# An adaLN block with attention: another list for its first stage, statistics partly on ScalarE, rows of ones by transfers, own banks for block 0's turns, twelve groups

## The chip, the core and the metric

The kernel runs on one core of a Trainium2 chip. Five engines work side by side, each through its own queue in order: TensorE (PE in the rows; PEld is its weight load), VectorE (DVE), ScalarE (ACT), GpSimd (POOL) and SyncE (SP), which issues most transfers. What counts is the device time of one execution in microseconds, the median of several runs.

## What is computed

x has 2048 rows of 512. A condition vector c gives six rows of 512 that shift, scale and gate two halves: attention with 32 heads of 16, and a feed-forward layer of width 1792. Cut to what matters:

```python
mod = (silu(c) @ w_mod).reshape(1, 6, 1, -1)
sa, ca, ga, sb, cb, gb = (mod[:, i] for i in range(6))
h = layernorm(x) * (1 + ca) + sa
qkv = (h @ wqkv).reshape(B, S, 3, 32, 16)
q, k, v = qkv transposed to (3, B, 32, S, 16)
p = softmax(q @ k.T * 16 ** -0.5)          # rows of 2048
x = x + ga * ((p @ v) @ wo)
h = layernorm(x) * (1 + cb) + sb
x = x + gb * (gelu(h @ w1 + b1) @ w2 + b2)
```

## The kernel before, in words

Products are kept exact enough by splitting each fp32 operand into a high and a low part (hi and lo): a product of 512 rows is a *group* of twelve matmuls, eight with the high part of x and four with the low part. The 2048 rows are four blocks of 512.

The kernel has three stages. The **first stage** (about 108 us) norms x, shapes it by the condition, turns it, splits it, and multiplies enough of it by wqkv for the attention to start: 13 groups. From its middle on it also computes row maxima of the scores (tile `mx` on TensorE, reduced on VectorE to `mxp`), which the attention needs ahead of its exponentials. The **attention stage** runs in half-steps: four score matmuls (`e`), four maxima matmuls, four products with v (`pv`), and, on the other half of the array's rows, up to six matmuls of *background* work (`bg`): the groups that the first stage left over, the output projection and the feed-forward layers of the blocks whose attention is done (`block0`, `plan`, `work`). The **tail** does the rest of the background and block 3, on the whole array.

The order of the first stage is written out by hand in `SCRIPT` (line 44), a list of words that the loop at line 569 plays; a word issues its instructions on the engine that it names (.a ScalarE, .v VectorE, .g GpSimd), and each engine keeps that order. The words that the text uses, with block b, tile t, feature chunk f; w is 0 for q, 1 for k, 2 for v:

- Z, W, va, vb: loads of x, of a piece of wqkv, of two pieces of w_mod. hw, lw: high and low part of a weight piece.
- S bt: mean and variance of 128 rows. F, P: add eps, power -0.5 (GpSimd). B: the offset that ScalarE's norm needs. N bt: norm.
- pa, pb, c, ml, md: the modulation product in two halves, its copy, its turn, the columns `modc`.
- T bf: four turns of x into one bank. H bf: shape by `modc` into a tile h32. I, L: high and low part of it.
- G wkb: a group. A, R, D: high part, copy and low part of its result, O: the store, K, Q: loads of keys and queries laid out by heads. U, C: turn and copy of values.
- M: fills a key tile with ones (rows 48, 49 and 112, 113 of each are used as factors for the maxima). X queues two maxima matmuls, x plays a reduction. w: filler matmuls. om, lm: store and load of the maxima rows.

Banks of PSUM are handed out by rings: "pr" (banks 0 and 7) for turns and groups, "mx" for the maxima. A tile waits until the last reader of the one that it replaces is done; the first stage has four h32 tiles (`FIRST`). TensorE's clock is granted by the chip at one of two levels, 1.2 and 2.4 GHz.

Of the kernel before, what the change touches and what calls it, by code (L numbers as in the profile page):

```python
# [45 lines left out]
N02.v ml0 T00 md0 S12 T03 H00.a hw00.g S10 I00.a T01 lw00.g S11 H03.a H01.a bt I03.v hw10.g W01 S13 I01.a T02
lw10.g be F1 L01.v H02.a L03.g W11 L00.v I02.a S22 P1 L02.v G100 S21 B1 N10.a N11.g S20 G000 N13.a R100.v
N12.a A100.v S23 D100.g F2 S31 A000.a P2 O100 T12 D000.v B2 H12.a S30 O000 T10 N22.a I12.g N23.v T13 N20.a
H10.v hw01.g N21.a H13.v T11 I10.g lw01.v I13.a T22 L10.g L12.v H11.a W20 L13.v T20 H22.a I11.g hw11.v T21 K00
H20.a I22.g L11.v I20.a lw11.g T23 H21.v K10 S32 G101 I21.g Q0 H23.v L22.g I23.v Q1 L20.v L23.g G110 L21.v  # L50
A101.a S33 hw20.g lw20.v F3 D101.v P3 R110.a X0*2 O101 A110.a x X0 B3 G200 x D110.g N32.a x N30.a x N31.g O110
N33.a x*2 A200.a X0*2 x X0 G102 K01 x*2 K11 x*3 A102.a X0*2 x X1 T30 D102.v x O102 T32 H30.a x I30.g T33 H32.a
x I32.a x X0*2 H33.a x U200 x I33.g T31 x C200 x O200 K12 L30.g X0*2 x H31.a G010 x K02 I31.g x L32.g x*2
L33.g L31.v A010.a X0*3 x R010.a G103 x D010.g x*2 O010 x*2 R103.a X0*2 x X0 A103.a G203 x D103.g x*2 O103 x*2
A203.a X0*2 x X0 G201 x*4 K03 x A201.a X0*2 x X0 K13 U201 x*2 pa1 C201 x O201 va2 pb1 x*2 vb2 X0 c1.v X0*2 x
ml1 x G111 md1 x*4 A111.a X0*2 R111.v X0 G112 x D111.g x*2 O111 x*2 A112.a X0 x X0 R112.a pa2 x D112.g x pb2 x
O112 x c2.a X1*2 x X1 mb0 x om x mb1 me0.a x U203 me1.a x*2 C203 X1*2 x X1 O203 G202 x*3 lm x*2 A202.a w1 X1
w1 X1 x w1 X1 U202 x*2 C202 x O202 x*2
# [1164 lines left out]
```

## Time and profile before

| what | us |
|---|---|
| median of 3 runs (1736.97 to 1739.30) | 1738.71 |
| the profiled execution, its time | 1738.16 |
| its span, first to last instruction | 1736.3 |
| first stage | 0 to 107.8 |
| attention stage | 107.8 to 1614.2 |
| tail | 1614.2 to 1736.3 |
| busy: PE, DVE, ACT, POOL | 1710.8, 1375.2, 1241.8, 685.0 |

The shares of the whole span (PE 99%) hide that the stages have different limits, so they are read stage by stage. A row of the timeline is: start, duration, engine, line, operation, output and inputs, count, and in brackets how long the engine had been idle and who ended that. A matmul's duration runs from its issue to its result; the distance from one to the next is shorter, and the chain of waits shows that.

### The profile page before, as it was taken

Reading aid. Unit: us, or ns where it says so; the run is one execution under the profiler, and the core shown is the slowest. Engines: PE = TensorE matmul, PEld = TensorE weight load, DVE = VectorE, ACT = ScalarE, POOL = GpSimd, SP = SyncE. Lnnn points to the kernel's source line nnn. Section 1 sums busy time; section 2 is a strip of 40 time slices with the busy share of each in tenths; the row PEclk is TensorE's granted clock in tenths of the full one; section 3 lists DMA queues with packets and bytes.
Section 4 is the critical chain, followed back from the end, with each engine's and each line's share of the span. In section 5 each row is a group of like instructions: output and inputs, shape, how many; then the busy total and the mean of one; then the engine's idle time right before and its main releaser. Section 6 shows DMA issues by size and latency. Waiting matters only on the chain.

```text
span 1736.3 us, 32537 instructions
## 1 busy us (share of the span) xinstructions
PE 1710.8 (99%) x12121; PEld 891.1 (51%) x12121; DVE 1375.2 (79%) x2298; ACT 1241.8 (72%) x2379; POOL 685.0 (39%) x688
## 2 busy tenths in 40 slices
PE   7999999999999999999999999999999999999999
PEld 6654444444444444444445444444445444444777
DVE  7998888888888888888889888888888888860332
ACT  3357778778777778778777778777877778778231
POOL 7333434435121256404631356404631356525310
PEclk8999999999999999999999999999999999999999
DMA  8646776767447534335454444335364344323554
GB/s 292 205 142 200 221 218 182 236 179 223 125 136 206 125 86 117 94 85 136 113 168 106 124 114 105 94 81 166 100 174 114 101 132 114 97 66 111 195 156 166
DMA packets 137130, 251.90 MB, mean 145 GB/s; under 512 B 25854, under 2 KB 45324, under 8 KB 136972
## 3 DMA queue, kind: packets, MB, share of 16 engines
q1 hardware_dynamic: 135712, 248.19, 50.3%
q8 instruction: 96, 1.57, 0.4%
q10 hardware_dynamic: 1260, 1.63, 0.3%
q14 instruction: 62, 0.51, 0.1%
HBM read 188.49 MB, written 61.28 MB: 144 GB/s over the span
## 4 chain that ended last, share of the span: by engine, by line
PE 91%; DVE 4%; ACT 2%; POOL 1%; DMA 1%; issue 1%; SPq 0%; ACTq 0%; POOLq 0%; DVEq 0%
PE bg L274 46%; PE pv L667 29%; PE e L637 11%; PE mx L387 3%; DVE mxp L392 2%; ACT p L642 1%; PE pr L274 1%; PE o L274 1%; PE warm L438 1%; DVE hTlo L481 1%; DVE bst L235 0%; ACT h L849 0%; DMA qst<-m 0%; PE mx L333 0%; PE bg L847 0%
## 5 line engine op out<-in xcount | busy, mean ns | idle before, releaser
L392 DVE TENSOR_REDUCE mxp<-mx 128x1 f32<-128x512 f32 x2048 | 1269.4, 682 | 201.4 <-PE mx L387 182.5
L642 ACT ACTIVATE p<-e 128x512 f32<-128x512 f32 x2032 | 1064.4, 605 | 308.1 <-PE e L637 292.8
L387 PE MATMUL mx<-kh,qst 48*128 48x512 f32 x2048 | 873.3, 441 | 1.9 <-DVE mxp L392 0.4
L637 PE MATMUL e<-qst,kh 50*128 50x512 f32 x2032 | 754.6, 419 | 7.0 <-ACT p L642 6.3
L667 PE MATMUL pv<-p,vg 128*32 128x512 f32 x4096 | 546.6, 605 | 0.0
L637 PEld LDWEIGHTS e<-qst,kh 50*128 50x128 f32 x2032 | 373.7, 186 | 148.7 <-ACT p L642 141.8
L387 PEld LDWEIGHTS mx<-kh,qst 48*128 48x128 f32 x2048 | 368.6, 185 | 21.1 <-DVE mxp L392 16.2
L274 PE MATMUL bg<-w,g 64*128 64x512 f32 (+1 forms) x1044 | 277.8, 404 | 0.0
L274 PEld LDWEIGHTS bg<-w,g 64*128 64x128 f32 (+1 forms) x1044 | 183.0, 185 | 142.7 <-ACT p L642 103.3
L274 PE MATMUL bg<-pchi,w 64*128 64x512 f32 (+1 forms) x656 | 194.5, 416 | 2.1 <-ACT p L642 2.0
L274 PEld LDWEIGHTS bg<-pchi,w 64*128 64x128 f32 (+1 forms) x656 | 109.0, 184 | 150.3 <-ACT p L642 102.2
L274 PE MATMUL bg<-hThi,wqkv 64*128 64x512 f32 x560 | 167.4, 418 | 0.3 <-ACT p L642 0.3
L274 PEld LDWEIGHTS bg<-hThi,wqkv 64*128 64x128 f32 x560 | 92.8, 184 | 118.9 <-ACT p L642 106.3
L667 PEld LDWEIGHTS pv<-p,vg 128*32 128x32 f32 x4096 | 81.4, 108 | 125.4 <-issue 117.6
L884 POOL TENSOR_SCALAR s<-s 128x512 f32<-128x512 f32 x40 | 59.8, 1496 | 137.4 <-ACT s L882 127.0
L903 POOL TENSOR_TENSOR x<-y,x 128x512 f32<-128x512 f32 x28 | 35.9, 1281 | 144.3 <-ACT y L902 139.3
L274 PE MATMUL bg<-pclo,w 64*128 64x512 f32 (+1 forms) x328 | 88.6, 389 | 0.0
L872 DVE TENSOR_TENSOR g<-h,g 128x512 fp32r<-128x512 f32 x16 | 11.6, 723 | 91.5 <-PE bg L274 62.7
L274 PE MATMUL bg<-hTlo,wqkv 64*128 64x512 f32 x280 | 76.4, 392 | 0.0
L819 POOL TENSOR_TENSOR x<-y,x 128x512 f32<-128x512 f32 x12 | 15.4, 1282 | 140.9 <-ACT y L816 114.8
L274 PEld LDWEIGHTS bg<-pclo,w 64*128 64x128 f32 (+1 forms) x328 | 60.5, 184 | 12.3
L274 PE MATMUL bg<-wo,pchi 64*128 64x512 f32 x192 | 64.8, 417 | 0.0
(160 smaller groups left out, 1331.9 us busy)
## 6 DMA issues: line engine op xcount, KB each, us to landing
kh<-qk SPq DMA_DIRECT2D x256, 192.0 KB
w<-w1s SPq DMA_DIRECT2D x56, 512.0 KB
w<-w2s SPq DMA_DIRECT2D x53, 512.0 KB
vg<-v SPq DMA_DIRECT2D x64, 332.0 KB
qk<-parts SPq DMA_DIRECT2D x32, 512.0 KB
qst<-qk SPq DMA_DIRECT2D x64, 192.0 KB
qk<-parts SPq DMA_DIRECT2D x32, 256.0 KB
ou<-osb SPq DMA_DIRECT2D x32, 256.0 KB
```

What stands on the lines that cost most here:

```text
L274: return te.matmul(ps, term[0][r], term[1][r], start=i == 0, stop=i == n - 1)
L387: te.matmul(ps, qst[u][r0 : r0 + KR, p, qc * P : (qc + 1) * P], kh(u, kr // 2)[r0 : r0 + KR, p, (kr % 2) * TB : (kr % 2 + 1) * TB], start= ...
L392: ins = ve.tensor_reduce(mxp[u][:, hc, kr : kr + 1], ps, axis=AX.X, op=ALU.max, negate=True)
L438: te.matmul(warm[:, :P], ident, ident, start=True, stop=True)
L481: e.tensor_tensor(hT[b][1][:, f], keep.pop(("H", b, f)), hT[b][0][:, f].bitcast(F32), op=ALU.subtract)
L637: te.matmul(ps, kh(u, kc // 8)[r0 : r0 + KX, p, (kc % 8) * P : (kc % 8 + 1) * P], qst[u][r0 : r0 + KX, p], start=True, stop=True)
L642: saw(ac.activation(t, ps, AF.Exp, scale=SCALE))
L667: te.matmul(cur["ps"][32 * j : 32 * (j + 1)], vg[u][:, kc, j * VW : j * VW + 32], pt.pop(4 * s + j), start=kc == 0, stop=kc == NKC - 1)
L819: gp.tensor_tensor(x2[t], y, x2[t], op=ALU.add)
L872: ve.tensor_tensor(g[:, 1], h, g[:, 0].bitcast(F32), op=ALU.subtract)
L884: gp.tensor_scalar(s, s, 1.0, None, op0=ALU.add)
L903: later(4, lambda: gp.tensor_tensor(x2[t], y, x2[t], op=ALU.add))
```

## The change

The list is replaced by another one, and four pieces around it change. `S` takes an engine: on ScalarE it is a copy and a squaring of the rows, each with its sum, and a small scaling; its output goes to a scratch tile of h32. Of the sixteen, S10, S30 and S23 go to ScalarE. `M` is now two transfers of two rows each out of the key tile that is filled at the start, in place of a memset of the whole tile; three tiles are filled so. Block 0's turns take banks 1, 2, 5 and 6 of a ring of their own. G112 leaves the list, and `plan` takes it up as background work.

```diff
+S2 = D ** -0.5
 SCRIPT = """
-va0 vb0 Z1 W00 bl W10 Z2 S01 Z3 M3.g S02 S00 S03 M4.g M1.v pa0 w7 va1 F0 P0 pb0 w4 N01.g N00.v N03.v c0.a vb1
+va0 vb0 W00 Z1 bl Z3 W10 S00.v Z2 S01.v M1 M4 S02.v M3 S03.v F0 P0 B0 N00.a N02.v N03.v pa0 w7 N01.v T01 T03 T00 T02 pb0 w4
...
     ring("pr", (0, 7))
+    ring("t0", (1, 2, 5, 6))
...
+    def stat(b, t, e):
+
+        rows = xin[b][:, t]
+        if e is not ac:
+            return ln_stat(mv1[b], t, rows)
+        junk, m = stage("h32"), small.tile([P, 1], F32, tag="m1", name="m1")
+        ac.activation(junk, rows, AF.Copy, scale=S2 / D, accum_out=m)
+        ac.activation(junk, rows, AF.Square, scale=-S2, bias=m, accum_out=mv1[b][:, t, 1:2])
+        ac.activation(mv1[b][:, t, 0:1], m, AF.Copy, scale=1 / S2)
...
     def turn_x(b, f):
-        keep["T", b, f] = ps = take("pr")
+        keep["T", b, f] = ps = take("pr" if b else "t0")
...
+    def ones(i):
+        for r0 in (KR, 64 + KR):
+            sy.dma_start(khalf[i][r0 : r0 + 2].bitcast(F32), khalf[2][r0 : r0 + 2].bitcast(F32))
...
-        "S": lambda b, t: ln_stat(mv1[b], t, xin[b][:, t]), "F": add_eps, "P": power, "B": offset, "N": norm1,
+        "S": stat, "F": add_eps, "P": power, "B": offset, "N": norm1,
...
-        "M": lambda i, e: e.memset(khalf[i].bitcast(F32), 1.0),
-        "w": filler,
+        "M": ones, "w": filler,
...
-        plan = [(1, 1, [3]), (2, 1, [0, 1, 2, 3])]
+        plan = [(1, 1, [2, 3]), (2, 1, [0, 1, 2, 3])]
```

ScalarE's queue from its first modulate on, before (h is the shaped chunk, hThi its high part, xin the rows of x, of block 0 to 3 by their numbers 234, 295, 303, 308; parts and pf are copies of a group's result):

```order
L474 ACTIVATE h_374<-pr,modc 128x512
L190 ACTIVATE hThi_214<-h_374 128x512
L474 ACTIVATE h_390<-pr,modc 128x512
L474 ACTIVATE h_392<-pr,modc 128x512
L190 ACTIVATE hThi_214<-h_392 128x512
L563 ACTIVATE b_h<-pr 128x14
L474 ACTIVATE h_414<-pr,modc 128x512
L190 ACTIVATE hThi_214<-h_414 128x512
L461 ACTIVATE xin_295<-xin_295,nb,rs_257 128x512 x3
L190 ACTIVATE parts<-pr 128x512
L474 ACTIVATE h_491<-pr,modc 128x512
```

The same stretch after; block 1 is now xin_297, block 3 xin_301 and block 2 xin_308:

```order
L190 ACTIVATE hThi_214<-h_410 128x512
L455 ACTIVATE h_417,m_418<-xin_297 128x512
L456 ACTIVATE h_417,mv_253<-xin_297,m_418 128x512
L457 ACTIVATE mv_253<-m_418 128x1
L455 ACTIVATE h_440,m_441<-xin_301 128x512
L190 ACTIVATE pf<-pr 128x512
L190 ACTIVATE parts<-pr 128x512
L455 ACTIVATE h_462,m_463<-xin_308 128x512
L456 ACTIVATE h_462,mv_254<-xin_308,m_463 128x512
L457 ACTIVATE mv_254<-m_463 128x1
L473 ACTIVATE xin_297<-xin_297,nb,rs_257 128x512
L190 ACTIVATE parts<-pr 128x512
```

Three statistics stand where three norms of block 1 stood; of those norms one is left, behind the third statistic (the rows of the second that only repeat are left out).

TensorE's queue from the first group to the second batch of maxima, before (wqkv_232 is the piece of k, wqkv_221 that of q, wqkv_222 the second piece of k, wqkv_224 that of v; hThi and hTlo 214 to 217 are blocks 0 to 3 high):

```order
L274 MATMUL pr<-hThi_214,wqkv_232 128x512 x8
L274 MATMUL pr<-hThi_214,wqkv_221 128x512 x8
L468 MATMUL pr<-ident,xin_295 128x128 x16
L468 MATMUL pr<-ident,xin_303 128x128 x16
L274 MATMUL pr<-hThi_215,wqkv_232 128x512 x8
L274 MATMUL pr<-hThi_214,wqkv_222 128x512 x8
L387 MATMUL mx<-kh_189,qst 128x512 x6
L274 MATMUL pr<-hThi_214,wqkv_224 128x512 x8
```

and after:

```order
L230 MATMUL pr<-wm_197,s_m 32x512 x4
L447 MATMUL pr<-ident 128x128 x7
L480 MATMUL t_347<-ident,xin_234 128x128 x4
L230 MATMUL pr<-wm_198,s_m 32x512 x4
L274 MATMUL pr<-hThi_214,wqkv_221 128x512 x8
L274 MATMUL pr<-hThi_214,wqkv_232 128x512 x8
L480 MATMUL pr<-ident,xin_297 128x128 x16
L480 MATMUL pr<-ident,xin_308 128x128 x16
L274 MATMUL pr<-hThi_215,wqkv_232 128x512 x8
L388 MATMUL mx<-kh_189,qst 128x512 x6
L274 MATMUL pr<-hThi_216,wqkv_232 128x512 x8
```

Block 0's turns moved ahead of the second half of the modulation product, and G110 (wqkv_222) moved from before the first maxima to behind them (the four low-part matmuls of each group, and three more turns of block 0, are left out).

TensorE's queue where the tail begins, behind the last `pv`, before and after (pchi and pclo are the shaped rows of block 2, w a weight piece in the attention stage's ring of tiles, wt one in a tile that exists only in the tail):

```order
L667 MATMUL pv<-p,vg 32x512 x8
L274 MATMUL bg<-pchi_5322,w_22566 128x512 x8
L274 MATMUL bg<-pchi_5322,w_22629 128x512 x8
L274 MATMUL bg<-w_22693,g 128x512 x3
L274 MATMUL bg<-w_22754,g 128x512 x3
L274 MATMUL bg<-w_22814,g 128x512 x3
L274 MATMUL bg<-w_22875,g 128x512 x3
```

```order
L682 MATMUL pv<-p,vg 32x512 x8
L274 MATMUL bg<-pchi_5485,w_22642 128x512 x8
L274 MATMUL bg<-pchi_5485,w_22673 128x512 x8
L274 MATMUL bg<-pchi_5485,w_22734 128x512 x8
L274 MATMUL bg<-w_22794,g 128x512 x3
L274 MATMUL bg<-w_22855,g 128x512 x3
L274 MATMUL bg<-w_22915,g 128x512 x3
L274 MATMUL bg<-wt_22966,g 128x512 x3
```

The tail begins with three first-layer groups where it began with two, and the fourth weight piece behind them is one that is loaded in the tail (the low-part matmuls are left out).

## Rows read from the trace of the kernel before

**Rows 1.** Windows by stage: busy us (and count) by engine, then clock, DMA.

```profile
18.30:48.60 30.30, 22.90 (x96) 16.31 (x93) 29.25 (x50) 14.56 (x22) 26.89 (x25) 0.83 0.81 256
48.60:107.80 59.20, 58.25 (x293) 36.24 (x292) 55.89 (x95) 18.62 (x34) 15.83 (x17) 1.00 0.64 203
107.80:1614.20 1506.40, 1495.41 (x11105) 728.29 (x11104) 1240.25 (x2068) 1179.10 (x2279) 613.75 (x610) 1.00 0.49 136
1614.20:1736.30 122.10, 118.02 (x522) 96.04 (x520) 40.03 (x65) 27.43 (x41) 17.65 (x17) 1.00 0.52 183
```

**Rows 2.** Timeline of PE: turns, G101's high part, first maxima.

```profile
17.90 1.18 PE L468 MATMUL pr<-ident,xin 128*128 128x128 f32 x8
...
30.30 0.60 PE L468 MATMUL pr<-ident,xin 128*128 128x128 f32 x4
...
41.12 3.75 PE L274 MATMUL pr<-hThi,wqkv 128*128 128x512 f32 x8 [1.13 <-DVE h L476]
...
48.62 0.96 PE L387 MATMUL mx<-kh,qst 48*128 48x512 f32 x6
```

**Rows 3.** Timeline of DVE: a run of reductions.

```profile
58.14 7.85 DVE L392 TENSOR_REDUCE mxp<-mx 128x1 f32<-128x512 f32 x13
```

**Rows 4.** Chain of waits (start, us, what): one group, issue to issue.

```profile
71.33 3.00 PE pr L274 x12
```

**Rows 5.** Timelines of DVE and POOL: memsets of key tiles.

```profile
9.33 1.76 DVE L564 MEMSET kh<- 128x2048 f32 x1 [0.38 <-issue]
...
5.21 3.54 POOL L564 MEMSET kh<- 128x2048 f32 x2
```

**Rows 6.** Timeline of SP: the first weight load into a tile of the tail.

```profile
1621.38 0.38 SPq L782 DMA_DIRECT2D wt<-w2s  x1
```

**Rows 7.** Chain of waits: from the second modulation product to modc.

```profile
14.38 1.04 PE pr L230 x8
...
18.08 0.16 DVE modc L540
```

**Rows 8.** Groups, 18.3 to 48.6: count, busy us, mean ns, idle.

```profile
L235 DVE BATCH_NORM_STATS2 bst<-xin 128x6 f32<-128x512 f32 x12 | 8.1, 677 | 0.0
...
L481 POOL TENSOR_TENSOR hTlo<-h,hThi 128x512 fp32r<-128x512 f32 x4 | 6.3, 1586 | 0.8 <-PE pr L468 0.4 <-DVE hThi L192 0.4
...
L474 ACT ACTIVATE h<-pr,modc 128x512 f32<-128x512 f32 x8 | 6.0, 771 | 3.3 <-PE pr L468 2.5 <-POOL hTlo L481 0.7
...
L461 ACT ACTIVATE xin<-xin,nb,rs 128x512 f32<-128x512 f32 x6 | 4.5, 806 | 4.8 <-POOL nb L456 4.8
L192 POOL CAST hThi<-h 128x512 fp32r<-128x512 f32 x5 | 3.9, 797 | 0.0
...
L190 ACT ACTIVATE hThi<-h 128x512 fp32r<-128x512 f32 x5 | 3.2, 632 | 0.3
...
L476 DVE TENSOR_SCALAR h<-pr,modc 128x512 f32<-128x512 f32 x4 | 3.1, 798 | 0.0
...
L463 DVE TENSOR_SCALAR xin<-xin,mv,rs 128x512 f32<-128x512 f32 x1 | 0.5, 516 | 0.0
...
L563 ACT ACTIVATE b_h<-pr 128x14 f32<-128x14 f32 x1 | 0.2, 166 | 0.0
```

**Rows 9.** Windows of 2 us, PE alone: busy, clock, DMA.

```profile
32.00:34.00 2.00, 1.09 (x8) 1.00 1.02 381
...
42.00:44.00 2.00, 2.00 (x6) 0.50 1.06 227
...
46.00:48.00 2.00, 2.00 (x10) 1.00 0.01 3
```

**Rows 10.** Chain of waits: a store's landing, a load's landing.

```profile
48.52 4.65 DMA qk<-parts
...
54.03 3.46 DMA kh<-qk
```

**Rows 11.** Timeline of PE in the tail: full matmuls.

```profile
1619.80 11.72 PE L274 MATMUL bg<-w,g 128*128 128x512 f32 x51
```

More of the change, by code (lines that the diff above doesn't have):

```diff
@@ L44 @@
 SCRIPT = """
-va0 vb0 Z1 W00 bl W10 Z2 S01 Z3 M3.g S02 S00 S03 M4.g M1.v pa0 w7 va1 F0 P0 pb0 w4 N01.g N00.v N03.v c0.a vb1
[L46 to L58, printed above, removed]
+va0 vb0 W00 Z1 bl Z3 W10 S00.v Z2 S01.v M1 M4 S02.v M3 S03.v F0 P0 B0 N00.a N02.v N03.v pa0 w7 N01.v T01 T03 T00 T02 pb0 w4
+c0.v hw00.g ml0 lw00.g md0 H03.a H00.v H02.a I03.g W11 S13.v I00.a I02.g S11.v bt be L00.g L02.v H01.a S12.v I01.a
@@ new lines @@
+L03.g S10.a L01.v G000 S33.v hw10.g S30.a F1 S31.v P1 S32.v R000.a lw10.g A000.a F3 S21.v S23.a S20.v D000.g W20 G100
+S22.v B1 O000 F2 P2 N13.a N10.v N11.v N12.v N22.g A100.a N21.v T10 D100.v H10.a N20.v O100 T13 I10.a T12 N23.g H13.v
+Q0 H12.v I13.a T11 Q1 L10.v I12.a H11.a L13.g T20 L12.v T23 H20.a I11.v P3 H23.a K00 T22 H22.a I23.v T21 L11.g K10
+I22.a G101 I20.a L22.v B3 L23.g N32.a N33.v H21.a N30.v L20.g I21.a X0*2 x X0 N31.a x L21.g G102 R101.a x A101.a x
+D101.g x*2 hw20.g A102.a X0 O101 X0 x X0 R102.a T31 x D102.g H31.a x X0 x I31.a hw11.g O102 T30 x H30.a X0 x lw11.g
@@ new lines @@
+T32 x H32.a X1 K01 x T33 I30.g I32.a x W01 X1 H33.a x K11 G110 L30.g x I33.a K12 x L32.g x K02 x L31.g lw20.v R110.a
+X0 vb1 X0*2 va1 hw01.a x G201 A110.a lw01.g x*3 D110.g x*2 A201.a X0 L33.g O110 X0 x X0 G103 x*5 A103.a X0 R103.v X0*2
+x D103.g G200 x*2 O103 x*3 A200.a X0*2 x X0 pa1 x va2 x X0 pb1 x U200 c1.a K03 x X0 C200 x ml1 vb2 O200 x K13 x X0 x
+X0 G010 x*5 R010.a X0 md1 X0 x X0 A010.a pa2 x D010.g x X0 pb2 x O010 U201 c2.a x X0 x C201 mb1 x O201 x me1.a X0 x X0
+mb0 x*2 me0.a X0 x G111 x*4 R111.a A111.v X1*3 x D111.g om G202 x*2 O111 x*3 A202.a X1 lm X1 x X1 U202 x G203 C202 x*2
@@ L59 @@
+O202 x*2 A203.a w1 X1 w1 X1 x w1 X1 U203 x C203 x X1 x O203 x*4
 """
@@ L372, in block_kernel @@
     xc, red, mrows = [0, 0], {}, set()
-    xorder = [int(t[1]) for t in SCRIPT.split() if t[:2] in ("X0", "X1") for _ in range(int(t[3:] or 1))]
+    xorder = [int(t[1]) for t in SCRIPT.split() if t[:2] in ("X0", "X1", "y0", "y1")
+              for _ in range(int(t[3:]) if "*" in t else 1)]
     xorder = [(u, xorder[:n].count(u)) for n, u in enumerate(xorder)]
```

## The prediction

> **What bounds the kernel now.** I first cut the span into stages by the busy time of each engine [rows 1]. The attention stage (107.8 to 1614.2 us) and the tail behind it are TensorE's: 1495.4 of 1506.4 and 118.0 of 122.1 us busy. The change leaves their code alone but for one group, so what it can win lies in the first 107.8 us. There the bound moves. From 18.3 to 48.6 VectorE is busy 29.25 of 30.3 us and TensorE 22.9: the vector queue (statistics, norms, low parts) holds the first maxima matmul back, which comes at 48.62 [rows 2]. From there to 107.8 TensorE is busy 58.3 of 59.2 us and VectorE 55.9: a pass of 13 reductions at 0.604 us [rows 3] runs against groups of 3.00 us [rows 4], almost level. So the end of the first stage is the time of the first maxima matmul plus about 59 us, and each part of the change is asked what it does to either.
>
> **The change part by part.**
>
> *Rows of ones by transfers.* One memset of 1.76 us leaves VectorE and two of 3.54 us together leave GpSimd [rows 5]. Both ran before 12 us, while TensorE did warm-up matmuls and the first modulation product, so I cost the removal at nothing. The six transfers that replace them are issues of about 0.4 us on SyncE [rows 6], 2.4 in all, between the last input load and the loads of W11 and W20; those weights are first used after the first maxima, and the first store has to wait for G000's copies, at 31. What is behind them in the queue has time. If that cover were gone, the price is the 2.4 us.
>
> *Own banks for block 0's transposes.* TensorE now turns block 0 before the second modulation product instead of after it. Sixteen turns at 8 in 1.18 us are 2.3 us [rows 2]. The modulation columns (c, ml, md) followed that product by 3.9 us, from 14.38 to 18.24 [rows 7]; they come 2.3 us later, at 20.6. In return nothing of block 0 waits for a bank afterwards. From 20.6: two modulates on ScalarE, 2 x 0.77, to 22.1; two high casts on GpSimd, 2 x 0.80 one behind the other with the last, to 23.0; two low parts there, 2 x 1.59, to 26.2 [rows 8]. G000 has its last operand at 26.2 and ends at about 27; G100 waits for GpSimd to finish the split of its weights (lw10 is queued behind L03, hw10 and the block's power) and ends near 34. Before, both were done at 30.3, where the first turn of block 1 stands [rows 2].
>
> *Statistics by ScalarE.* S10.a, S30.a and S23.a take three statistics of 0.68 us, with their small aggregates, off VectorE (over 2 us) [rows 8] and put nine activations on ScalarE. Their scratch is an h32 tile, the fifth of four, so S10.a can't begin before L03 on GpSimd has read the oldest: 26.2. The price of one is in no row. Below it stand a copy of 0.63, a squaring with a bias like the norm's 0.81 and a tiny one of 0.17, 1.61 us; above, twice the first two, 3.05. I take the lower end and two more tiny activations for the two sums, 1.95, since nothing but the sum is added to known work. Then S10 ends at 28.2, S30 at 30.1, two copies out of G000 at 31.3, S23 at 33.3. VectorE's queue waits with it: block 2's add of eps stands ahead of block 1's three norms, so these end at 33.5 + 3 x 0.52 = 35.1 [rows 8]. T10 starts at 35.2, 4.9 us later than now.
>
> *The turn of blocks 1 and 2.* Before, it took from 30.3 to 41.1, where G101 starts [rows 2]; it was fed by a vector queue that also did weights, copies and statistics. In the new list it is a chain through two banks: G100's bank is free at 36.4 (one norm and D100 on VectorE), a turn 0.6, H13 and H12 on VectorE 2 x 0.80, a cast 0.63, four modulates on ScalarE 4 x 0.77: 42.3. G101 then takes 3.0 us at 2.4 GHz [rows 4]; now its first eight matmuls alone take 3.75 [rows 2], because the granted clock was 0.50, 1.2 GHz, after a stretch with little but turns, and was back to 1.00 at 46 [rows 9]. Its price is 3.0 or 4.75; I take the middle, and the first maxima matmul follows at once, without G110 between: 46.2. Its first quarter of K is there in time: stored at 36.5, landed 4.65 later, loaded in 0.8 + 3.46 [rows 10], 45.8.
>
> The clock is the place where a page speaks against the list. By the steps above TensorE gets two gaps of over 3 us, before G000 (from about 19.5) and inside G100 (to 31); in the trace of before it kept 2.4 GHz through a thin stretch up to 34 [rows 9]. The Trainium skill, TensorE: Matmul & The Clock Gate, section "HAM oscillation", says that bursts of matmuls with waits between them each start at half clock. By that rule G000 and G100 would run at 1.2 GHz too, by the row they would not; the second is the only one that anything waits for, and the sum differs by the 2.4 us below.
>
> *The stage behind it.* The same nine groups remain (G110 moved in, G112 out), two fillers fewer. TensorE's own work is 58.3 less 0.8, or 57.5. VectorE's is 88 x 0.604 = 53.2 and some 2.7 of other pieces (four of about 0.68), 55.9. Between these I put 57.0; 55.9 is the least, 59.2 the most. The first attention matmul comes at 46.2 + 57.0 = 103.2, 4.6 us sooner.
>
> *Twelve groups.* The thirteenth, G112, becomes the first background group of the attention stage. The order of instructions shows 511 half-steps of the same make-up before and after (448 with six background, four maxima and four score matmuls, and the same rest): the background work fills every half-step to the end, so the group comes out behind, as 468 instead of 456 full matmuls in the tail. Attention: 0, between -1.5 and +1.5 for what moves by four half-steps. Tail: 12 x 11.72/51 = 2.8 us [rows 11], all on the path. A tail that starts with three first-layer groups also reaches a weight loaded in the tail sooner: its load was issued 7.2 us after the tail's start [rows 6], and is needed after 45 matmuls, 10.3 us. With a landing of 3.46 to 4.65 [rows 10] TensorE waits 0.3 to 1.5; I take 0.7.
>
> **Sum.** -4.6 + 2.8 + 0.7 = -1.1 us. Against the profiled execution (span 1736.3, time 1738.16) that is 1737.1; the median of the runs shown is 0.55 above that execution. I predict 1737.0.
>
> **The rivals.** *The vector queue is the only bound* (faster). For it: VectorE is busy 96% of the stretch before the maxima, and loses about 8 us of work there. Statistics at 1.61 bring S23 and all behind it 1.0 forward, G101 at 2.4 GHz another 0.9, and the stage runs at VectorE's 55.9: first score at 44.3 + 55.9 = 100.2. That is -7.6 + 2.8 + 0.4 = -4.4, 1733.8. Against it: three of its steps wait for ScalarE or GpSimd. *ScalarE becomes the bound* (slower). At 3.05 us for a statistic the third ends 3.3 later, norms, turns and G101 with it, and G101 runs at 1.2 GHz (0.9): first score at 46.2 + 4.2 + 58 = 108.4, so +0.6 + 3.5 = +4.1, 1742.3. It decides from a statistic of about 2.6 us. Against it: the copies and the squares themselves have rows. *Low clock from G000 on.* By the rows, G000 and G100 at 0.47 a matmul (3.75/8) instead of 0.25 are 2.6 us longer each; G000 hides behind S30, G100 shows 1.5, and G101 0.9: 1739.5. For it the two gaps, against it the full clock through a thin stretch up to 34. *The list does not do what it says*, since the group comes back in the tail: that is inside the forecast.
>
> **How the numbers follow.** Forecast 0.46, vector bound 0.27, low clock 0.15, ScalarE bound 0.12. A measurement of this kernel tells about 0.2% (3.5 us) from no change. The forecast and the low clock lie within it: 0.61. Faster 0.27, slower 0.12. The forecast's own range is 1735 to 1739.5 (statistics and clock 1.9, stage 1.2, tail 0.8). With the vector bound's 1733.8 and half of the slow case inside, the range is 1732.8 to 1741.2.
>
> **What would show it.** modc at 20.6 and S10.a at 26 on ScalarE (right: the banks cost 2.3, the scratch tile holds); a statistic under 1.7 or over 2.6 decides between the rivals; the first maxima matmul at 46 (44 or 50 for the rivals); the granted clock during G100 and G101; first score matmul at 103; half-steps of unchanged length; the tail 2.8 us longer with a wait before the first wt matmul. The forecast is wrong if the attention stage changes by more than 1.5 us, which no step here explains.

## The result: 7.5 us slower, and where they are

The changed kernel takes 1746.13 us (median of 4, 1745.48 to 1747.96), the kernel before 1738.62: a ratio of 1.0047, 95% interval 1.0034 to 1.0060. The forecast was 1737.0 with a range up to 1741.2; it is outside, and on the other side of no change.

The spans of the two profiled executions are 1743.9 and 1736.3. The 7.6 us between them, stage by stage (first maxima matmul, first score matmul and last product with v are read from each trace):

| | before | after | difference | forecast |
|---|---|---|---|---|
| first maxima matmul | 48.62 | 46.37 | -2.25 | -2.4 |
| from there to the first score matmul | 59.49 | 63.15 | +3.66 | -2.2 |
| attention, to the last product with v | 1506.17 | 1505.15 | -1.0 | 0 |
| tail, to the last matmul | 118.48 | 124.37 | +5.9 | +3.5 |
| from the last matmul to the end | 3.59 | 4.89 | +1.3 | 0 |

So the part that the change is mostly about did what was forecast, and the stage behind it, the tail and the end didn't. The windows by stage of the changed kernel answer to [rows 1] (busy us and count of PE, PEld, DVE, ACT, POOL; granted clock, DMA share, GB/s):

```profile
18.30:46.30 28.00, 20.46 (x85) 14.52 (x85) 23.40 (x41) 20.04 (x39) 23.36 (x21) 0.82 0.69 197
46.30:109.20 62.90, 58.94 (x289) 36.05 (x288) 56.17 (x95) 19.16 (x35) 19.39 (x18) 1.00 0.69 211
109.20:1614.60 1505.40, 1495.46 (x11104) 729.02 (x11105) 1239.67 (x2068) 1178.94 (x2279) 610.19 (x605) 1.00 0.49 136
1614.60:1743.90 129.30, 122.14 (x534) 98.23 (x532) 40.70 (x66) 28.79 (x43) 17.97 (x17) 0.99 0.52 181
```

Ahead of the maxima VectorE went from 29.25 of 30.3 us to 23.4 of 28, and ScalarE from 14.6 to 20.0: the work did move. In the second row the work of TensorE and VectorE is what it was, 58.9 and 56.2 us, and yet the stage is 3.7 us longer. Neither engine fills it: TensorE stands idle for 4 us. The timeline of PE says for what; the first three rows answer to [rows 2]:

```profile
33.02 1.30 PE L480 MATMUL pr<-ident,xin 128*128 128x128 f32 x4 [0.37 <-issue]
...
42.24 3.28 PE L274 MATMUL pr<-hThi,wqkv 128*128 128x512 f32 x8
...
46.37 0.97 PE L388 MATMUL mx<-kh,qst 48*128 48x512 f32 x6
...
83.45 1.05 PE L388 MATMUL mx<-kh,qst 48*128 48x512 f32 x6 [2.27 <-DMA kh<-qk]
...
87.31 1.06 PE L230 MATMUL pr<-wm,s_m 128*32 128x512 f32 x8 [1.38 <-DMA wm<-in_w_mod_dram]
```

Two waits for transfers, 2.27 us for a quarter of K and 1.38 for a piece of the modulation weights, 3.65 together. The trace of before has neither. SyncE's timeline of the changed kernel shows how they come about:

```profile
59.23 1.31 SPq L172 DMA_DIRECT2D wm<-in_w_mod_dram  x2
...
74.16 0.37 SPq L172 DMA_DIRECT2D wm<-in_w_mod_dram  x1
75.55 0.94 SPq L360 DMA_DIRECT2D kh<-qk  x2
76.59 0.60 SPq L172 DMA_DIRECT2D wm<-in_w_mod_dram  x1
77.25 1.07 SPq L360 DMA_DIRECT2D kh<-qk  x2
```

The new list loads the second pair of modulation pieces (va1, vb1; 1 MB each) at 59 us, where the list before loaded it behind the first modulation product, at 15. The last pair (va2, vb2) follows at 74.16 and 76.59, the first as soon as its half of the second product has read the tile it replaces, the second behind a quarter of K in the queue. In the list before, all four transfers of the two K quarters (K03, K13) stood ahead of that pair:

```profile
76.24 1.91 SPq L360 DMA_DIRECT2D kh<-qk  x4
80.75 1.25 SPq L172 DMA_DIRECT2D wm<-in_w_mod_dram  x2
```

Now one piece stands ahead of each quarter. The quarter of K that TensorE waits for is the one issued at 75.55, between the two: it is there 7.9 us later, where [rows 10] shows 3.46 for such a load. vb2 is behind both, and the chain of waits gives its landing:

```profile
76.59 10.68 DMA wm<-in_w_mod_dram
```

The windows of before (first two rows) and after show it as the share of the transfer engines and as idle time of PE:

```profile
60.00:72.00 12.00, 11.89 (x53) 7.69 (x53) 12.00 (x21) 4.69 (x9) 7.14 (x7) 1.00 0.62 199
78.00:87.00 9.00, 8.81 (x55) 5.14 (x54) 8.56 (x16) 1.26 (x3) 0.00 (x0) 1.00 0.97 275
```

```profile
60.00:72.00 12.00, 12.00 (x56) 7.98 (x52) 11.30 (x20) 3.44 (x6) 5.33 (x4) 1.00 1.05 308
78.00:87.00 9.00, 5.67 (x30) 3.17 (x28) 6.10 (x13) 1.08 (x2) 1.26 (x1) 1.00 1.06 298
```

From 60 to 72 the transfer engines are busy at a share of 1.05 instead of 0.62, and from 78 to 87 TensorE works 5.67 of 9 us instead of 8.81. The first of these, the second pair with the K loads and stores beside it, is over before the waits begin. The share is 0.36 in the 2 us window of the changed kernel (PE alone) in which va2 and the quarter that TensorE waits for are issued:

```profile
74.00:76.00 2.00, 2.00 (x18) 1.00 0.36 102
```

In the tail the table of waits of PE has two new entries (line, what was waited for, us, times, longest):

```profile
PE o L274 <- DMA wo<-wos: 1.5, 1, 1.5
...
PE bg L274 <- DMA wt<-w2s: 0.3, 1, 0.3
```

The second is the wait that was forecast; the first, for a piece of the output projection's weights, was not.

### The profile page after: what moved, and what is told of

Its sections match the earlier page's. It is cut to its first block, busy times and chain, and to the rows that moved or that the text cites. A ratio compares the mean times of both kernels' runs of the same rounds, so it can differ in the third digit from the quotient of the medians.

```text
span 1743.9 us, 32542 instructions
## 1 busy us (share of the span) xinstructions
PE 1712.8 (98%) x12117; PEld 891.5 (51%) x12117; DVE 1368.4 (78%) x2288; ACT 1249.2 (72%) x2398; POOL 678.6 (39%) x681
## 4 chain that ended last, share of the span: by engine, by line
PE 93%; DMA 2%; DVE 2%; ACT 2%; POOL 1%; issue 0%; SPq 0%; ACTq 0%; DVEq 0%; POOLq 0%
PE bg L274 44%; PE pv L682 29%; PE e L652 11%; PE mx L388 5%; DVE mxp L393 1%; PE pr L274 1%; DMA wm<-in_w_mod_dram 1%; ACT p L657 1%; PE o L274 1%; DMA wo<-wos 0%; ACT h L864 0%; PE bg L862 0%; PE mx L333 0%; DMA wt<-w2s 0%; PE pr L230 0%
## 5 line engine op out<-in xcount | busy, mean ns | idle before, releaser
L274 PE MATMUL bg<-w,g 64*128 64x512 f32 (+1 forms) x1020 | 272.3, 404 | 0.0
L274 PEld LDWEIGHTS bg<-w,g 64*128 64x128 f32 (+1 forms) x1020 | 178.5, 185 | 142.3 <-ACT p L657 102.5
L274 PEld LDWEIGHTS bg<-pchi,w 64*128 64x128 f32 (+1 forms) x648 | 107.8, 184 | 144.5 <-ACT p L657 98.6
L274 PE MATMUL bg<-hThi,wqkv 64*128 64x512 f32 x576 | 172.3, 418 | 0.5 <-ACT p L657 0.4
```

Of the source, the lines that this page charges most:

```text
L274: return te.matmul(ps, term[0][r], term[1][r], start=i == 0, stop=i == n - 1)
```

## The experiments

The theory: the first stage lost its gain to transfers behind one another (theory A), and the tail pays for the thirteenth group with twelve matmuls and with waits for weights. The rivals: the reductions on VectorE set the stage's length anyway, so that the waits only lie in time that is lost in any case; and the tail's length has another cause.

Each ratio is to executions of the kernel before beside that run, whose median lay between 1737.58 and 1738.62. The five columns behind it come from the trace of one execution each, which can lie off the median: that of e3 took 1745.67 us, of e4 1742.34, of e6 1751.28, of e14 1742.02. The last column is where the granted clock was 0.5 between the first maxima matmul and the first score matmul, from windows of 2 us.

| run | median us | ratio to before, 95% | first maxima | first score | between | tail, TensorE | half clock |
|---|---|---|---|---|---|---|---|
| before | 1738.62 | 1 | 48.62 | 108.11 | 59.49 | 118.48 | none |
| after | 1746.13 | 1.0047 [1.0034, 1.0060] | 46.37 | 109.52 | 63.15 | 124.37 | none |
| e1, small gate loads | 1742.41 | 1.0026 [1.0015, 1.0037] | 45.46 | 104.81 | 59.34 | 124.44 | none |
| e2, order rewritten | 1745.96 | 1.0049 [1.0032, 1.0066] | 47.15 | 109.36 | 62.21 | 124.70 | none |
| e9, loads early | 1747.98 | 1.0054 [1.0041, 1.0066] | 46.89 | 111.30 | 64.41 | 124.63 | 77 to 87 |
| e13, early, in place | 1748.60 | 1.0062 [1.0049, 1.0076] | 45.80 | 112.35 | 66.55 | 124.62 | 84 to 92 |
| e3, before, twelve groups | 1743.88 | 1.0040 [1.0025, 1.0055] | 46.15 | 110.66 | 64.52 | 123.98 | 83 to 100 |
| e4, after, thirteen | 1744.92 | 1.0042 [1.0027, 1.0057] | 46.04 | 111.16 | 65.13 | 119.60 | none |
| e5, memsets | 1743.38 | 1.0033 [1.0022, 1.0043] | 45.58 | 107.31 | 61.73 | 124.83 | none |
| e6, statistics on VectorE | 1749.29 | 1.0061 [1.0043, 1.0079] | 48.42 | 114.95 | 66.53 | 125.83 | 87 to 97 |
| e7, turns in the shared banks | 1744.22 | 1.0039 [1.0023, 1.0054] | 45.05 | 107.05 | 62.00 | 126.71 | none |
| e8, before, statistics on ScalarE | 1738.73 | 1.0005 [0.9996, 1.0015] | 47.73 | 106.89 | 59.17 | 119.14 | none |
| e10, list with thirteen, loads early | 1741.85 | 1.0019 [1.0011, 1.0028] | 46.62 | 111.97 | 65.36 | 119.04 | 79 to 85 |
| e11, the same with fillers | 1742.76 | 1.0024 [1.0015, 1.0033] | 45.62 | 111.08 | 65.46 | 119.07 | 77 to 83 |
| e12, before with fillers | 1737.36 | 0.9994 [0.9985, 1.0003] | 46.28 | 106.25 | 59.97 | 118.50 | none |
| e14, before, fillers and statistics | 1739.37 | 1.0010 [1.0001, 1.0019] | 48.09 | 109.09 | 60.99 | 119.13 | 83 to 87 |

### Are the two waits transfers behind one another? (e1, e13)

e1 takes the cost away without moving an instruction: of the last pair of modulation pieces only a quarter of the columns is loaded. The second pair stays whole and where it is.

```diff
     def load_wm(i, slot, q=sy):
-        q.dma_start(wslot[slot], wm_r[:, :, i * D : (i + 1) * D])
+        n = P if i in (2, 5) else D
+        q.dma_start(wslot[slot][:, :, :n], wm_r[:, :, i * D : i * D + n])
```

> The changed kernel, but of the last two pieces of the modulation weights (1 MB each) only the first quarter of the columns is loaded, so the gates come out wrong; no instruction moves on any engine. In the changed kernel TensorE waits 2.27 us for a quarter of K at 83.45 and 1.38 us for the last modulation piece at 87.31. Theory A (these two waits are transfers behind one another: the two pieces of 1 MB share the transfer engines with the K loads issued beside them): both waits shrink to under 0.3 us, the first score matmul comes at about 106 instead of 109.5, and the whole is 3.0 to 3.7 us shorter. Rival B (the reductions on VectorE bound the stage anyway and the waits only lie on top of its idle time): the waits go, but the first score matmul moves by less than 1 us.

Measured: 3.7 us less than the changed kernel in the medians (all of its executions, 1741.42 to 1743.06, lie below all of the changed kernel's, 1745.48 to 1747.96), and 3.81 us less between first maxima and first score matmul (59.34 for 63.15). Both waits are gone; the timeline of PE over the same instructions, and the window that held 5.67 us of PE:

```profile
80.28 0.97 PE L389 MATMUL mx<-kh,qst 48*128 48x512 f32 x6
81.18 1.07 PE L231 MATMUL pr<-wm,s_m 128*32 128x512 f32 x8
```

```profile
78.00:87.00 9.00, 9.00 (x49) 4.03 (x47) 8.40 (x17) 2.90 (x6) 1.28 (x1) 1.00 0.73 233
```

TensorE is busy 9.00 of 9 us. That is theory A with its number, and the rival, under 1 us, is out. (The first score matmul comes 4.7 us sooner in this trace; the other 0.9 lies ahead of the first maxima matmul, where G101 ran at full clock in e1 and not in the changed kernel.) It also says which transfers they are: the last pair, which stands ahead of K. The second pair, moved from 15 to 59 us, is loaded in e1 as in the changed kernel, and the stage is as long as before the change.

e13 is the same cost the other way. It was meant as a mend: the second pair of pieces loaded at 22 us, the last pair behind the second product, then the K quarters.

```diff
-... I03.g W11 S13.v ... X0 vb1 X0*2 va1 hw01.a x G201 ...
+... I03.g va1 vb1 W11 S13.v ... X0 X0*2 hw01.a x G201 ...
-... X0 pa1 x va2 x X0 pb1 x U200 c1.a K03 x X0 C200 x ml1 vb2 O200 x K13 x X0 x ...
+... X0 pa1 pb1 x va2 vb2 x X0 x U200 c1.a K03 K13 x X0 C200 x ml1 O200 x x X0 x ...
```

> As the run with the loads taken early, but with the second modulation product left where the changed kernel has it (both halves behind one another), so that no stretch of maxima matmuls stands alone; the second pair of modulation pieces is loaded at 22 us, the last pair right behind that product, then both K quarters. Theory (the gain of the early loads was eaten by a half clock that began in the stretch where TensorE waited for reductions): granted clock 1.00 from 48 to the first score matmul, the waits for transfers at most 1 to 2 us in sum instead of 3.65, stage 60 to 61.5 us, whole 1743.5 to 1745. Rival (the half clock comes with early loads as such, or without any cause in the list): clock 0.50 somewhere between 70 and 100, stage above 63 us.

SyncE issues both pieces, and all four transfers of K behind them; PE's timeline shows what that does:

```profile
73.56 1.24 SPq L172 DMA_DIRECT2D wm<-in_w_mod_dram  x2
74.91 2.38 SPq L360 DMA_DIRECT2D kh<-qk  x4
```

```profile
84.61 1.45 PE L388 MATMUL mx<-kh,qst 48*128 48x512 f32 x6 [4.15 <-DMA kh<-qk]
85.99 1.94 PE L230 MATMUL pr<-wm,s_m 128*32 128x512 f32 x8
```

With 2 MB ahead of K instead of one, K is there 9.7 us after its issue (74.91 to 84.61), the wait for it is 4.15 us instead of 2.27, and the one for the modulation weights is gone. My expectation (at most 1 to 2 us of waits) had forgotten the very thing that the case is about: it put both pieces ahead of K in the queue. What it shows is that the wait follows what stands ahead of K, and that loading the second pair early doesn't take it away. The same quarter takes 7.1 us from issue to use in e2 (below) and 7.9 in the changed kernel, each with 1 MB ahead of it, 6.8 to 7.4 with the same load order in e4 to e7, and 9.7 with 2 MB ahead (e13); a quarter with no such piece ahead took 3.46 [rows 10]. The Trainium skill, DMA: Bandwidth & Descriptors, section "Queues, rings and completion order", says that the transfers of one issuing engine go into one ring on each transfer engine and are taken up in ring order. The traces agree, by these numbers. No run puts both quarters ahead of the first piece, as the list before has them, with all else of the new list in place. The second row above is also the price of a clock: eight matmuls of the modulation product take 1.94 us where the changed kernel takes 1.06, since the granted clock fell to 0.50 at 85.24, 0.6 us after TensorE started again.

### Two mends that move the wait (e2, e9)

e2 puts the last K quarter (K13) ahead of the last piece, and G111 with its copies ahead of the last modulation product. e9 puts the early loads of e13 together with a second modulation product ahead of G103, so that the last pair is loaded from 66 us on.

```diff
-... c1.a K03 x X0 C200 x ml1 vb2 O200 x K13 x ... X0 A010.a pa2 x D010.g x X0 pb2 x O010 U201 ... G111 x*4 R111.a A111.v ...
+... c1.a K03 K13 x X0 C200 x ml1 vb2 O200 x x ... X0 A010.a G111 x D010.g x X0 R111.a A111.v x D111.g O010 pa2 x ...
```

```diff
-... O110 X0 x X0 G103 x*5 A103.a ... X0 pa1 x va2 x X0 pb1 x U200 c1.a K03 x ... ml1 vb2 O200 x K13 x ...
+... O110 X0 x X0 pa1 pb1 va2 vb2 c1.a G103 x*5 A103.a ... X0 x x X0 x U200 K03 K13 x ... ml1 O200 x x ...
```

> The changed kernel with the order around the last modulation step rewritten: the K quarter of the second unit is queued ahead of the last modulation piece, and the group G111 with its copies stands ahead of the last modulation product, which gives its weights about 5 us more. Nothing is left out. Theory A: both waits for transfers go, first score matmul at 106 to 107, whole 2.5 to 3.7 us shorter than the changed kernel (about 1742.5 to 1743.5). Rival B: less than 1 us.

> The changed kernel with nothing left out, but with the second pair of modulation pieces loaded at about 22 us, where the transfer engines are idle (24 to 30 us), the second modulation product and the loads of the last pair ahead of G103 (about 65 us instead of 74 to 77), and both K quarters directly behind one another. If the two waits for transfers in the changed kernel are transfers behind one another, both go as they did with the quarter-size loads: stage from first maxima to first score matmul 59 to 60 us instead of 63.2, whole 3 to 4 us shorter than the changed kernel, about 1742.5. Rival (the reductions take the place of the waits): stage above 62 us, whole within 1.5 us of the changed kernel.

Neither gained. In e2 the wait for the weights is gone; the quarter that is waited for, K03, still stands behind the first piece, and its wait is still 1.18 us. VectorE's timeline has a new one, too: the copy A111, now early in its queue, waits for ScalarE's copy of the same result, and thirteen reductions stand behind it.

```profile
87.93 0.69 DVE L192 CAST parts<-pr 128x512 fp32r<-128x512 f32 x1 [2.39 <-ACT pf L190]
```

In e9 no wait for a transfer is left at all, and the stage is 64.4 us, longer than the changed kernel's. PE's timeline:

```profile
73.75 2.93 PE L388 MATMUL mx<-kh,qst 48*128 48x512 f32 x8
76.61 1.11 PE L333 MATMUL pr<-ident,vr 128*128 128x128 f32 x4
...
81.33 3.78 PE L274 MATMUL pr<-hThi,wqkv 128*128 128x512 f32 x8
84.91 1.91 PE L274 MATMUL pr<-hTlo,wqkv 128*128 128x512 f32 x4
```

With the product moved ahead, eight maxima matmuls stand by themselves and wait for reductions (2.93 us, 0.37 each, where six take 0.97 elsewhere); behind them everything runs at half speed up to 87 us, G010 in 5.4 us instead of 3.0. So here the wait for transfers was replaced by a half clock, and not in this execution alone: the mean granted clock of e9's five executions is 0.992 to 0.994, that of the changed kernel's four 0.995 to 0.996. Whether those lonely maxima matmuls bring the clock down was the question to e13, and it doesn't settle it: e13 has no such stretch, and the clock fell there too, behind a wait of 4.15 us. In the changed kernel it did not fall behind 2.27 us.

### The thirteenth group (e3, e4)

```diff
-... X0 G112 x D111.g x*2 O111 x*2 A112.a X0 x X0 R112.a pa2 x D112.g x pb2 x O112 x c2.a ...
+... X0 x D111.g x*2 O111 x*2 X0 x X0 pa2 x x pb2 x x c2.a ...
-        plan = [(1, 1, [3]), (2, 1, [0, 1, 2, 3])]
+        plan = [(1, 1, [2, 3]), (2, 1, [0, 1, 2, 3])]
```

That is e3, on the kernel before. e4 does the reverse to the changed kernel:

```diff
-... om G202 x*2 O111 x*3 A202.a X1 lm X1 x X1 U202 ...
+... om G112 x*2 O111 x*2 A112.a R112.a x G202 X1 D112.g A202.a O112 lm X1 x X1 U202 ...
-        plan = [(1, 1, [2, 3]), (2, 1, [0, 1, 2, 3])]
+        plan = [(1, 1, [3]), (2, 1, [0, 1, 2, 3])]
```

> The kernel before with one edit: G112 leaves the list and is taken up as background work, as in the changed kernel. Theory A (the tail pays for the moved group: 12 matmuls, 2.75 us, and about 2 us of waits for weights loaded in the tail, and the first stage wins little since VectorE's reductions bound it): tail 5 to 7 us longer, first score matmul 0.5 to 3 us earlier, whole +2 to +6 us. Rival B (the tail's +7 us in the changed kernel are something else, for example run-to-run, and the group costs its 2.8 us and saves 3.0): whole between -1.5 and +1.

> The changed kernel with G112 back in the list, behind G111, and out of the background work. Theory A: the tail is back at 122 to 123 us (7 shorter), the first score matmul 2 to 3.5 us later than the changed kernel's 109.5; whole 3.5 to 5.5 us shorter than the changed kernel, about 1741 to 1742.5. Rival B (the tail's length is not the group's): tail stays above 127 us and the whole gets 0 to 3 us longer.

The tail is the group's: 123.98 us with it in e3 (118.48 before), 119.60 without it in e4 (124.37 after). Over all runs the tails with twelve groups are 124.0 to 126.7, with thirteen 118.5 to 119.6. The two longest, e6's and e7's, hold 3.4 us of half clock each. Of some 5.5 us, 2.75 are the twelve matmuls, and the table of waits of e3 has the same two entries as the changed kernel, in a kernel that has nothing else of the change:

```profile
PE o L274 <- DMA wo<-wos: 1.3, 1, 1.3
PE bg L274 <- DMA wt<-w2s: 0.7, 1, 0.7
```

That leaves 0.8 us in e3 to which no row gives a name. What the group costs or saves in the first stage these two don't say. The first score matmul came 2.55 us later in e3, where I expected it sooner; its clock was 0.50 between 83 and 100 us. The first score matmul came 1.6 us later in e4 (expected 2 to 3.5), and e4's median, 1744.92, is 1.2 us under the changed kernel's, where 3.5 to 5.5 were expected, and not clearly apart from it.

### The other parts (e5, e6, e7, e8)

The edits, in this order: memsets of the key tiles again; the three statistics of the changed kernel back on VectorE; block 0's turns behind the second product and in the shared banks; and, in the kernel before, four statistics on ScalarE.

```diff
-... M1 M4 S02.v M3 S03.v ...
+... M1.v M4.g S02.v M3.g S03.v ...
-        "M": ones,
+        "M": lambda i, e: e.memset(khalf[i].bitcast(F32), 1.0),
```

```diff
-... L03.g S10.a ... S30.a ... S23.a ...
+... L03.g S10.v ... S30.v ... S23.v ...
```

```diff
-... N01.v T01 T03 T00 T02 pb0 w4 c0.v hw00.g ml0 lw00.g md0 H03.a H00.v H02.a ...
+... N01.v pb0 w4 c0.v hw00.g ml0 T03 lw00.g md0 T00 H03.a H00.v T02 T01 H02.a ...
-        keep["T", b, f] = ps = take("pr" if b else "t0")
+        keep["T", b, f] = ps = take("pr")
```

```diff
-... I02.a S22 P1 ... S21 B1 ... S32 G101 ... S33 hw20.g ...
+... I02.a S22.a P1 ... S21.a B1 ... S32.a G101 ... S33.a hw20.g ...
```

> The changed kernel with the rows of ones filled by memsets again (one on VectorE, two on GpSimd) in place of six transfers. Theory: both ways lie beside the wait for the first modulation weights; the loads of W11 and W20 are issued about 7 us sooner, but nothing before the first maxima matmul uses them: first maxima matmul within 0.5 us of the changed kernel's 46.4, whole within 1.5 us. Rival: the six issues (7.03 us on SyncE) hold back the weight loads that GpSimd's splits and with them the block's power wait for: first maxima matmul 1 to 2 us earlier, whole as much shorter.

> The changed kernel with the three statistics S10, S30 and S23 back on VectorE, at the same places of the list. Theory (VectorE's queue up to the norms of block 1 is the bound there): VectorE takes 3 x 0.79 us more ahead of them, the first turn of block 1 comes at 35 instead of 33.0, first maxima matmul 1.5 to 2.4 us later, whole 1.5 to 2.5 us longer. Rival (the turn phase is held by its two banks and by the two norms of block 2 on GpSimd, which end at 38.4): first maxima matmul within 0.7 us, whole within 1 us.

> The changed kernel with block 0's turns behind the second modulation product again and in the two banks that turns and groups share, as in the kernel before. Theory: the modulation columns come 2.1 us sooner (18.2 instead of 20.3), but the third and fourth turn wait for a bank; G000 ends within 1 us of the changed kernel's 27.9 and the first maxima matmul within 1 us of 46.4. Rival (the 2.1 us are on the path): first maxima matmul 1.5 to 2.1 us sooner.

> The kernel before with one part of the change: four statistics (S22, S21, S32, S33) go to ScalarE, where it is idle in the trace of before (23.5 to 27.3 and 40 to 45.9), each at 1.67 us as in the changed kernel. Theory (VectorE's queue alone holds the first maxima matmul): 4 x 0.79 = 3.2 us leave it, first maxima matmul 1.5 to 3 us earlier than 48.6, whole 1.5 to 3 us shorter than before. Rival (the turn phase is a chain through two banks whatever VectorE has left to do): whole within 1 us.

e6 is clear in the trace: without the three statistics on ScalarE the first turn of block 1 comes at 35.66 instead of 33.02, G101 starts at 44.57 instead of 42.24, and the first maxima matmul comes at 48.42 instead of 46.37, 2.05 later. So in this list they are worth 2 us there. Its whole, 3.2 us longer in the median, is not a price of the statistics alone: the traced execution holds a half clock from 87 to 97, and the four spread from 1745.15 us at a mean clock of 0.997 to 1751.58 at 0.993. In the kernel before (e8) four of them are worth 0.9 us at the first maxima matmul (1.5 to 3 were expected) and nothing that the whole shows (1.0005, 0.9996 to 1.0015): VectorE waits 2.49 us for a low part on GpSimd there, so it was not the only bound. e5 and e7 came out 2.8 and 1.9 us under the changed kernel, with wide ranges (1742.47 to 1746.39 and 1743.88 to 1747.07). Their first maxima matmuls come 0.8 and 1.3 us sooner, which fits neither the theory nor the rival that I had put on record for either. In their traces the wait for K is 1.0 us each instead of 2.27. The intervals overlap with the changed kernel's, so I don't put a price on the transfers or the banks; that either helps is not shown.

### The list without its losses, and fillers (e10, e11, e12, e14)

e10 puts thirteen groups, memsets and e9's loads into the changed kernel; e11 adds four filler matmuls behind seven of the eight turns of blocks 1 and 2, into a bank that is free there. e12 adds the same fillers to the kernel before, and e14 also e8's statistics.

```diff
-    def filler(n):
-        ps = take("pr")
+    def filler(n, ring="pr"):
+        ps = take(ring)
...
-        "w": filler,
+        "w": filler, "f": lambda n: filler(n, "t0"),
...
-... T12 D000.v ... T10 N22.a ... T13 N20.a ...
+... T12 f4 D000.v ... T10 f4 N22.a ... T13 f4 N20.a ...
```

> The same, and G112 back in the list and the rows of ones by memsets, so that of the change the other list, the three statistics on ScalarE and block 0's own banks are left. From the runs so far: first maxima matmul 45.5, stage 59.3 plus 1.6 to 3 for the thirteenth group, first score matmul 106.5 to 108 (before 108.1), tail 122 to 123 like before: whole 1737 to 1739, level with the kernel before or up to 1.5 us under it. If the thirteenth group costs the first stage more than the 5.5 us that it costs the tail, it comes out above 1741.

> The same as the run with thirteen groups, and four filler matmuls of 128 columns into a bank that is free there behind each of seven of the eight turns of blocks 1 and 2. If the half clock of G101 comes from the thin stretch of turns ahead of it, the granted clock stays at 1.00 from 33 to 46 and G101's first eight matmuls take 2.1 us instead of 3.3 to 3.75: first maxima matmul 1 to 1.5 us sooner, whole as much shorter. If not, or if the fillers (0.5 us each) only delay the turns: whole within 0.5 us or up to 1.5 us longer.

> The kernel before with nothing of the change, but with the same fillers behind seven of the turns of blocks 1 and 2. In its trace the clock is 0.50 from 34.7 to 44.95 and G101's first eight matmuls take 3.75 us. If the thin stretch is the cause: clock 1.00 there, first maxima matmul at about 46.5 to 47 instead of 48.6, whole 1 to 2 us shorter than before. If the fillers delay the turns instead: 0 to 1.5 us longer.

> The kernel before with the four statistics on ScalarE and the fillers behind seven turns, both together. Alone they moved the first maxima matmul from 48.6 to 47.7 and 46.3, and the whole by +0.3 and -1.1 us. If they add up: clock 1.00 from 33 to 46, first maxima matmul at 45 to 45.5, first score matmul at 105 to 105.5, whole 1735 to 1736.5, faster than both kernels. If the chain of turns through two banks sets the time once the clock is full: as with fillers alone, 1737 to 1738.

e10 has neither the group in the tail nor a wait for transfers, and is still 0.19% over the kernel before (0.11 to 0.28%): 65.4 us from first maxima to first score matmul (60.9 to 62.3 expected), with a half clock from 79 to 85, so it doesn't tell what the thirteenth group costs. The fillers do what they should to the clock: in e11 and e12 it is 1.00 from 30 to 46, in e12 in the whole first stage. The mean clock of e12's eleven executions is 0.998 to 1.000, that of the kernel before beside them 0.995 to 0.999. In e12 G101's first eight matmuls take 2.11 us (3.75 before) and the first maxima matmul comes at 46.28 (48.62 before, [rows 2]). These rows of e12 answer to [rows 9]:

```profile
34.00:36.00 2.00, 2.00 (x20) 1.00 0.64 240
...
42.00:44.00 2.00, 2.00 (x10) 1.00 1.06 213
```

In the medians that is 1.07 us, within the uncertainty. e11's first maxima matmul comes 1.0 us sooner than e10's, as expected, and its median is 0.9 us longer, within the intervals. In e14 the two don't add up, in the median (1739.37, where 1735 to 1736.5 was expected) or in the trace, which is of an execution 2.65 us above it: the clock is 0.50 from about 23 to 29 there, G000 and G100 end 2 us later than in e12, and the packed turns (0.44 us of turn and 0.89 of fillers each; I had put the fillers at 0.5) start at 31.44 instead of 29.45 and end as much later. No version here is clearly faster than the kernel before.

## Why the prediction was wrong, point by point

**Up to the first maxima matmul the number was right, in part by luck: two errors cancel.** modc was done at 20.5 (forecast 20.6). S10 did not wait for GpSimd's second low part of block 0, which ended at 25.64 (forecast 26.2): it began at 23.98, right behind ScalarE's own last cast, so that its scratch tile held it is not shown. A statistic is these five rows of ScalarE's timeline, 1.67 us (forecast 1.95, lower bound 1.61):

```profile
23.98 0.63 ACT L455 ACTIVATE h<-xin 128x512 f32<-128x512 f32 x1
24.52 0.19 ACT L455 ACTIVATION_READ_ACCUMULATOR h<-xin 128x1 f32 x1
24.74 0.72 ACT L456 ACTIVATE h<-xin,m 128x512 f32<-128x512 f32 x1
25.37 0.18 ACT L456 ACTIVATION_READ_ACCUMULATOR h<-xin,m 128x1 f32 x1
25.46 0.19 ACT L457 ACTIVATE mv<-m 128x1 f32<-128x1 f32 x1
```

So the third ended at 30.94 instead of 33.3, and VectorE, with statistics of its own until 32.20, came to block 2's add of eps only at 32.30: its own queue held the norms of block 1, not ScalarE. T10 came at 33.02 instead of 35.2. Then the turns took 9.2 us instead of 7.1, because a chain that I built of ScalarE and VectorE alone leaves out GpSimd, which does two norms of block 2 there (POOL's timeline: 2.2 us each) before the low part that frees a tile:

```profile
33.98 4.42 POOL L475 TENSOR_SCALAR xin<-xin,mv,rs 128x512 f32<-128x512 f32 x2
38.37 1.48 POOL L493 TENSOR_TENSOR hTlo<-h,hThi 128x512 fp32r<-128x512 f32 x1
```

G101 at 42.24 (forecast 42.3), 3.95 us long by the chain of waits (forecast 3.0 or 4.75, taken in the middle), first maxima matmul at 46.37 (46.2). Smaller slips: the terms for the first quarter of K make 45.4, not 45.8; the first score matmul of before is at 108.11, and the sum counts from 107.8; its 1737.1 was not raised by the 0.55 us by which the median lay above the traced execution. The six issues for the rows of ones took 7.03 us on SyncE, not 2.4; what they cost is not settled (e5).

**The stage behind it is the step that failed**: 57.0 forecast, between 55.9 and 59.2, and 63.15 measured. Two errors are in it. 3.8 us are the transfers (e1), for which the sum has no term. The prediction counted the DMAs of the words that the diff adds (ones) and of what stands behind these in the queue, W11, W20 and the stores; it says nothing of va1, vb1, va2 and vb2, 4 MB in all. Of these the last pair is the loss: it stood behind both K quarters and now stands ahead of them, one piece each. The words stand in the two lists for anyone to compare, and the windows of before show a share of 0.97 from 78 to 87. That the second pair moves as well, from 15 to 59 us, is not shown to cost anything: e1 leaves it there and has no wait, and e13 takes it back to 22 us and waits longer. The other 2.3 us are a term set too low by method: I put the stage between TensorE's sum of work, 57.5, and VectorE's, 55.9, as if the longer of two nearly level queues could run without a wait for the other. The kernel before takes 59.49 us with 58.25 and 55.89 us of work [rows 1], e1 takes 59.34, and the 0.8 us that I took off TensorE's sum did not show either (58.94 in the changed kernel). The stage before it was the better measure of the stage after.

**Attention** was forecast at 0 within 1.5 and is -1.0. In all sixteen kernels it is 1504.6 to 1506.9 us.

**The tail** was forecast at +3.5. The 2.8 for the matmuls hold (2.75 by the distances between them); the wait for the first weight loaded in the tail is there with 0.3 us by the table (0.7 forecast). Missing was a second wait, 1.5 us for the output projection's weights: the shift by one group pushes them, too, into loads that are issued in the tail, and I followed only the first such load. e3 measures the group at +5.5 us of tail, so moving it was a loss of which the first stage would have had to win back all. Of the 5.9 us here some 1.3 have no row of waits.

**The rivals.** None of the three was the one. The low clock came for G000 (0.50 from about 20.8 to 27.7) and for most of G101's high part, but not for G100:

```profile
22.00:24.00 2.00, 1.19 (x2) 0.50 0.88 283
24.00:26.00 2.00, 1.99 (x5) 0.50 0.37 84
...
28.00:30.00 2.00, 0.68 (x4) 1.00 0.00 0
```

G000 ran at half clock behind an idle 2.27 us, G100's other seven matmuls at 2.4 GHz behind an idle 1.32 us. By the rule that the prediction cited from the Trainium skill, TensorE: Matmul & The Clock Gate, section "HAM oscillation", bursts with waits between them start at half clock; the trace agrees for G000 and not for G100. The cost was as priced: nothing for G000, since VectorE came to its add of eps later than ScalarE's third statistic, and about 0.9 for G101. A statistic of 1.67 us was the sign for the rival with the vector queue as the only bound; its first maxima matmul at 44 did not come, since GpSimd's norms stand in the turns. That ScalarE or VectorE would bound the stage behind the maxima was not in question; that the transfers would, no rival said.

**The end.** 1.3 us of the 7.6 lie between the last matmul and the end: VectorE's last addition starts at 1739.08 of 1743.9 in the changed kernel, at 1732.80 of 1736.3 before.

```profile
1739.08 0.69 DVE L914 TENSOR_TENSOR x2t<-bg,x2t 128x512 f32<-128x512 f32 x1 [2.03 <-PE bg L274]
```

What follows is one store of 256 KB; from its issue to the end it is 2.8 us in before and 4.1 in the changed kernel. The longer time stands in after, e1, e2, e8, e9, e13 and e14 (4.8 to 4.9 us from the last matmul to the end), the shorter in the others (3.6 to 3.7), with twelve groups and with thirteen. What decides it was not found.

## What to carry to other kernels

When a list of instructions is replaced, go through the large transfers first: where each was issued, where it is issued now, what is in flight beside it and which small load now stands behind it. Two pieces of 1 MB put ahead of two K quarters cost 3.8 us here, more than the 2.25 that all the work moved between engines gained; 2 MB issued 45 us later, with nothing waiting behind them, are not shown to cost anything. For the length of a stage in which two engines are nearly level, take the measured stage of the kernel before and change it by differences, not the larger of two sums. A mend that takes a wait away is worth what the next wait leaves of it: e2, e9 and e13 each took one or both of these waits away, and each got another wait, a longer one or a half clock in its place.

## What was not expected of the hardware

The granted clock of the first stage is not fixed by the order of the work. In e3, on TensorE the same instructions in the same order as in the kernel before up to 86 us, it was 1.00 from 30 to 46, where before shows 0.50 from 34.7 to 44.95, and 0.50 from 83 to 100 but for 3.4 us between, where before shows 1.00. Seven of the sixteen traces have 3 to 14 us of such a clock between 76 and 100; in e13 it follows 4.15 us without a matmul, in e9 a stretch of waiting maxima matmuls, and in e3 neither. It nearly doubles what it covers: the sixteen matmuls of the last modulation product take 3.64 us in e3 and 1.92 before.

```profile
91.21 3.64 PE L230 MATMUL pr<-wm,s_m 128*32 128x512 f32 x16
```

Why the clock fell in e3 stays open. A comparison of two first stages within some 4 us therefore needs the clock of both beside it.
